# Strassen in the second channel product, affine parts moved, and batch 0 pipelined by head pair, in an attention and ResMLP kernel

## The chip, the cores and the metric

The kernel runs on one core of one Trainium2 chip. The metric is the device time of one execution in microseconds (us), as a median over runs. The span in a profile is some 2 us shorter than that time, since it starts at the core's first instruction. Runs over 1.5% above the fastest of the same kernel are named where they occurred; they count in the medians quoted and not in the ratios.

## The reference

Input q, k, v are 4 batches x 8 heads x 768 tokens x 64. A sorting matrix `P` (8x8 for each head, normalised five times by rows and columns) mixes the 8 blocks of k and v. Attention within each block follows, and its output (768 x 512 for a batch) goes through a ResMLP block.

```python
for _ in range(5):                       # P = sort_net
    P = np.exp(P - P.max(-1, keepdims=True))
    P = P / P.sum(-1, keepdims=True); P = P / P.sum(-2, keepdims=True)
k_sorted = np.einsum('bhij,bhjcd->bhicd', P, k_b)      # v in the same way
x = softmax(scale * q_b @ k_sb^T) @ v_sb               # per block of 96 tokens
a1  = alpha1 * x + beta1
u   = x + lam * np.einsum('ts,bsd->btd', w_tok, a1)    # token mixing, 768 x 768
a2  = alpha2 * u + beta2
out = u + lam * (np.maximum(a2 @ w_ch1, 0.0) @ w_ch2)  # 512 -> 2048 -> 512
```

`lam` is about 0.01, so the channel product contributes little to the output.

## The kernel before

TensorE (`pe`) multiplies, ScalarE (`act`) does the exponentials and ReLUs, VectorE (`dve`) does most evictions (copies of results out of PSUM, where TensorE writes). In the traces below sc_ps are the scores, et their exponentials, x_ps is et times v (`Vs`), k_ps and q_ps are k and q on their way to kT and qT, tok_ps is token mixing, and h_ps and ch_ps are the two channel products. Tokens are kept in tiles of 128, of which 96 rows come from the first six blocks and 32 from the last two. `w_tok` must be transposed with its columns in that order. The kernel before sorts them on VectorE and then transposes full tiles of 128 columns:

```python
def sort_wtok(n):
    ...
    for lo, hi, base in ((0, 96, 0), (96, 128, TAIL)):     # two copies on VectorE
        dve.tensor_copy(t_[:, :, :, lo:hi], wt16[...])

def prep_wtok(which, eng):
    for ks in which:
        pst = psb([128, S], F16, "wtok_ps")
        for tt in range(NT):
            pe.transpose(pst[:, tt * 128:(tt + 1) * 128], wtp[ks // 2][:, tt, ks % 2, :], ident16[:])
        eng(w_tokT[:, ks, :], pst[:])
```

The channel part works on halves of 384 tokens. The first product (`h_ps`) needs a ReLU on ScalarE for each result, the second (`ch_ps`) needs two VectorE operations for each tile of 128 tokens:

```python
def moe_h(b, hf, which=range(HT)):
    for m in which:
        hps = psb([128, 384], FT, "h_ps")
        for ci in range(CT):
            pe.matmul(hps[:], W1p[:, ci, m*128:(m+1)*128], a2T_of[b][hf][:, ci, :], ...)
        act.activation(hT_of[(b, hf)][m], hps[:], AF.Relu)

def moe_ch(b, hf, kks=range(3)):
    ...
        for m in range(HT):
            pe.matmul(cps[:], hT[m][:, kk*128:(kk+1)*128], W2p[:, m, lo:hi], ...)
        dve.tensor_tensor(cps[:], cps[:], lamB[:, lo:hi], ALU.mult)
        dve.tensor_tensor(ost[:, lo:hi], cps[:], u_of[b][kt][:, lo:hi], ALU.add)
```

Where batch 1's attention is prepared, channel products of batch 0 stand between its k and q pieces:

```python
for kk in range(2):
    moe_ch(0, 0, (kk,))
    mix_k(1, gs=((0, 1), (2,))[kk])
    for h4 in range(2 * kk, 2 * kk + 2):
        turn_q(1, h4, dve.tensor_copy)
```

The softmax here doesn't subtract the row's maximum and nothing guards it: scores larger than these inputs give would overflow.

## Time and profile before

| | before |
|---|---|
| median of the first 3 runs | 268.65 us |
| span of the profiled run | 266.8 us |
| TensorE / VectorE / ScalarE busy | 96% / 58% / 47% |
| start of first h_ps (end of the head) | 42.47 us |
| token mixing of batches 1, 2, 3 starts at | 85.09, 143.86, 202.64 us |

I use these points as stage boundaries throughout. "Head" is all before the first h_ps; stage 2 runs from there to token mixing of batch 1; stages 3 and 4 end at token mixing of batches 2 and 3; the last stage ends with the last matmul.

A timeline line gives start, duration, engine, line, operation, names, shapes and count.

```profile
25.55 0.51 PE L65 MATMUL wtok_ps<-ident,wtp 128*128 128x128 f16 x6
```

A run of matmuls lasts 0.16 us beyond its stream (a record of 512 columns lasts 379 ns, and in a full stream the next one starts after 216), so the six here take (0.51 - 0.16) / 6 = 0.058 us each. All 36 cost 3.0 us.

The same timeline in stage 2, and the window around it (stretch, length, then busy time of PE, PEld, DVE, ACT, POOL, then granted clock, DMA share and GB/s):

```profile
55.03 2.75 PE L65 MATMUL ch_ps<-W2p,hTa 128*128 128x512 bf16 x11
57.62 1.03 PE L65 MATMUL ch_ps<-W2p,hTb 128*128 128x512 bf16 x4
58.49 1.06 PE L65 MATMUL k_ps<-bigP,raw 128*128 128x128 f16 x16
59.48 1.00 PE L65 MATMUL q_ps<-ident,qn 128*64 128x128 f16 x24
60.41 2.76 PE L65 MATMUL ch_ps<-W2p,hTa 128*128 128x512 bf16 x11
```

### The profile page before, as it was taken

How to read it: one execution, taken by the hardware profiler on the slowest of the kernel's cores; microseconds unless marked ns; L12 is line 12 of the kernel's file. 1: busy time of each engine (PE TensorE's matmuls, PEld its weight loads, DVE VectorE, ACT ScalarE, POOL GpSimd, SP SyncE). 2: the span in 40 equal slices, each digit the busy share in tenths (PEclk: the TensorE clock that was granted, in tenths of full speed). 3: DMA queues.
4: the chain of work that ended last, by engine and by line, in shares of the span. 5: the costliest groups of instructions: out<-in, count | busy, mean ns of one | idle time of the engine just before them, and what ended most of it. 6: DMA issues, size and time to landing. Idle time of an engine off the chain costs nothing.

```text
span 266.8 us, 5147 instructions
## 1 busy us (share of the span) xinstructions
PE 257.3 (96%) x2049; PEld 141.6 (53%) x2059; DVE 154.8 (58%) x333; ACT 125.8 (47%) x232; POOL 92.6 (35%) x100
## 2 busy tenths in 40 slices
PE   7799999999999999999999999999999999999993
PEld 3467745565565444554565444554565445545542
DVE  6878687639567966722585867704675962042033
ACT  3376767642585312980375404970474305505600
POOL 8524789103585615008918125002409000000000
PEclk9999999999999999999999999999999999999999
DMA  6999999989999544499996342492200422012012
GB/s 80 183 208 252 206 211 207 209 209 118 206 165 146 115 83 120 115 83 95 207 196 135 61 100 80 118 109 51 81 1 2 86 71 79 2 39 79 2 39 79
DMA packets 62423, 30.88 MB, mean 116 GB/s; under 512 B 48888, under 2 KB 58112, under 8 KB 62400
## 3 DMA queue, kind: packets, MB, share of 16 engines
q0 software_dynamic: 23024, 15.60, 39.1%
q1 hardware_dynamic: 39376, 14.96, 32.7%
q8 instruction: 16, 0.26, 0.4%
q14 instruction: 7, 0.06, 0.1%
HBM read 32.78 MB, written 8.65 MB: 155 GB/s over the span
## 4 chain that ended last, share of the span: by engine, by line
PE 89%; ACT 4%; DVE 4%; issue 1%; DMA 1%; DVEq 0%; ACTq 0%
PE ch_ps L65 31%; PE h_ps L65 30%; PE tok_ps L65 12%; PE x_ps L65 5%; PE sc_ps L65 4%; ACT kT L65 2%; PE v_ps L65 2%; PE k_ps L65 1%; PE q_ps L65 1%; ACT et L65 1%; DVE csum L65 1%; DVE P L65 1%; PE m_ps L65 1%; DVE rsum L65 1%; PE wtok_ps L65 1%
## 5 line engine op out<-in xcount | busy, mean ns | idle before, releaser
L65 PE MATMUL h_ps<-a2T,W1p 128*128 128x384 bf16 x512 | 93.4, 326 | 0.2
L65 ACT ACTIVATE hTa<-h_ps 128x384 bf16<-128x384 f32 x96 | 45.9, 492 | 67.7 <-PE h_ps L65 66.6
L65 PE MATMUL ch_ps<-W2p,hTa 128*128 128x512 bf16 (+2 forms) x290 | 65.9, 370 | 0.5
L65 PEld LDWEIGHTS <-W1p 128*128 128x128 bf16 x512 | 47.5, 98 | 30.3 <-issue 0.9
L65 DVE TENSOR_TENSOR ch_ps<-ch_ps,lamB 128x512 f32<-128x512 f32 (+2 forms) x25 | 16.9, 676 | 62.8 <-PE ch_ps L65 60.1
L65 POOL TENSOR_SCALAR u<-b1lB,rs 128x512 f32<-128x512 f32 x18 | 28.9, 1612 | 64.7 <-DVE ost L65 60.1
L65 PEld LDWEIGHTS <-hTa 128*128 128x128 bf16 x300 | 28.7, 98 | 32.4
L65 PE MATMUL tok_ps<-x,w_tokT 128*128 128x512 f16 x144 | 32.1, 379 | 0.0
L65 POOL TENSOR_TENSOR u<-x,u 128x512 f32<-128x512 f16 x22 | 25.4, 1190 | 18.2 <-DVE x L65 17.3
L65 ACT ACTIVATE et<-sc_ps 96x768 f16<-96x768 f32 x32 | 24.9, 807 | 11.7 <-PE sc_ps L65 11.7
L65 ACT CAST u<-u 128x512 f16<-128x512 f32 x24 | 14.8, 618 | 25.7 <-DVE u L65 25.7
L65 PE MATMUL ch_ps<-W2p,hTb 128*128 128x512 bf16 (+2 forms) x100 | 25.0, 371 | 0.0
L65 PEld LDWEIGHTS <-w_tokT 128*128 128x128 f16 x180 | 14.8, 97 | 16.1
L65 DVE TENSOR_TENSOR tok_ps<-tok_ps,a1lB 128x512 f32<-128x512 f32 x24 | 16.6, 693 | 7.7 <-PE tok_ps L65 7.6
L65 DVE CAST kT<-k_ps 64x512 f16<-64x512 f32 x24 | 16.5, 688 | 3.4 <-PE k_ps L65 3.0
L65 DVE TENSOR_TENSOR x<-x_ps,recip 96x512 f16<-96x512 f32 (+2 forms) x32 | 17.6, 554 | 0.9
L65 DVE TENSOR_TENSOR u<-tok_ps,u 128x512 f32<-128x512 f32 x24 | 16.4, 689 | 1.7
L65 ACT ACTIVATE hTb<-h_ps 128x384 bf16<-128x384 f32 x32 | 15.3, 497 | 3.8 <-PE h_ps L65 3.4
L65 DVE TENSOR_TENSOR ost<-ch_ps,u 128x512 f32<-128x512 f32 (+2 forms) x25 | 16.6, 665 | 0.6
L65 POOL DMA_DIRECT2D qn<-in_q_dram x18 | 15.4, 872 | 4.2 <-PE q_ps L65 3.4
L65 PEld LDWEIGHTS <-hTb 128*128 128x128 bf16 x100 | 9.6, 98 | 10.9
L65 PEld LDWEIGHTS <-et 96*128 96x128 f16 (+2 forms) x288 | 12.4, 99 | 4.6 <-issue 1.2
(95 smaller groups left out, 214.0 us busy)
## 6 DMA issues: line engine op xcount, KB each, us to landing
out_dram<-ost SPq DMA_DIRECT2D x23, 192.0 KB, 2.2
raw<-in_v_dram POOLq DMA_DIRECT2D x8, 384.0 KB, 8.2
raw<-in_k_dram POOLq DMA_DIRECT2D x8, 384.0 KB, 10.7
vscr<-vA SPq DMA_DIRECT2D x6, 384.0 KB, 4.4
Vs<-vscr SPq DMA_DIRECT2D x6, 384.0 KB, 7.5
W1p<-in_moe_w_ch_dram POOLq DMA_DIRECT2D x4, 512.0 KB, 10.5
W2p<-in_moe_w_ch_dram POOLq DMA_DIRECT2D x4, 512.0 KB, 18.6
qn<-in_q_dram POOLq DMA_DIRECT2D x12, 128.0 KB, 5.8
```

The source lines that it names most:

```text
L65: ins = getattr(self.eng, name)(*args, **kwargs)
```

## The change

Its intent is to save columns on TensorE: two tiles of tokens become one Strassen product of seven block products instead of eight. The sums of hT blocks and the seven evictions go to VectorE. `lam` is folded into W2, alpha2 into W1, beta2 into a bias of the ReLU, and alpha1 and beta1 are applied to x before token mixing. Batch 0's attention is pipelined by head pair. The operands of both channel products become f16 instead of bf16. The sorting copies of `w_tok` go, and each tile is transposed in two parts, 96 and 32 columns, instead. The core of the diff:

```diff
-    def sort_wtok(n):
...
     def prep_wtok(which, eng):
         for ks in which:
             pst = psb([128, S], F16, "wtok_ps")
             for tt in range(NT):
-                pe.transpose(pst[:, tt * 128:(tt + 1) * 128], wtp[ks // 2][:, tt, ks % 2, :], ident16[:])
+                cols = slice(tt * 128, (tt + 1) * 128)
+                pe.transpose(pst[0:96, cols], wt16[:, tt, 96 * ks:96 * ks + 96], ident16[:])
+                pe.transpose(pst[96:128, cols], wt16[:, tt, TAIL + 32 * ks:TAIL + 32 * ks + 32], ident16[:])
             eng(w_tokT[:, ks, :], pst[:])
...
-    spin(psb([128, 512], FT, "spin_ps")[:], 7)
+    spin(psb([128, 512], FT, "spin_ps")[:], 12)
...
+    def affine(b, lo, hi, eng, kts=slice(0, NT)):
+        eng.tensor_tensor(xa, x, a1l16[...], ALU.mult)
+        eng.tensor_tensor(xa, xa, b1l16[...], ALU.add)
...
+    def moe_h(b, th, which=range(MH)):            # thirds of 256 tokens
+            for mm in range(2):
+                act.activation(hT[:, m, :], hps[:, mm, :], AF.Relu, bias=hbias[:, m:m + 1])
...
+    def moe_sums(b, th):                          # four sums of 128x1024, f16
+        dve.tensor_tensor(S1, A21, A22, ALU.add)
+        dve.tensor_tensor(S2, S1, A11, ALU.subtract)
+        dve.tensor_tensor(A21, A11, A21, ALU.subtract)
+        dve.tensor_tensor(S4, A12, S2, ALU.subtract)
...
+        product(pa, A11, B11, True, False)        # 8 matmuls of 256 columns each
+        take(u11, pa)                             # u += ps / 1024 on VectorE
+        product(pb, A12, B21, True, True)
+        take(u11, pb)
+        product(pa, S2, T2, False, False)
+        take(u12, pa)
...                                               # four more
...
+    for n in range(3):
+        mix_k(1, gs=(n,), share=(2, 0, 2))
+        turn_q(1, n, act.copy)
+        moe_h(0, 1, range(2 + n, 3 + n))
+    turn_q(1, 3, act.copy)
+    for n in range(4):
+        scale_w2(n)                               # 4 x 2048 elements on VectorE
+    combine_w2()                                  # 4 x 2048 elements on VectorE
```

## The prediction

> **What bounds the kernel now.** I read the page first (busy shares, then the chain that ended last), then the timeline of TensorE, then the windows between the points that the timeline gives, then the groups by form for durations.
>
> ```profile
> PE 257.3 (96%) x2049; PEld 141.6 (53%) x2059; DVE 154.8 (58%) x333; ACT 125.8 (47%) x232; POOL 92.6 (35%) x100
> ...
> PE 89%; ACT 4%; DVE 4%; issue 1%; DMA 1%; DVEq 0%; ACTq 0%
> ```
>
> TensorE is busy 96% of the span and is 89% of the chain, mostly ch_ps (31%), h_ps (30%) and tok_ps (12%). So matmul columns are the currency, as long as nobody makes TensorE wait. The timeline of TensorE shows the rate and the stages:
>
> ```profile
> 42.47 4.06 PE L65 MATMUL h_ps<-a2T,W1p 128*128 128x384 bf16 x24
> ...
> 85.09 7.93 PE L65 MATMUL tok_ps<-x,w_tokT 128*128 128x512 f16 x36
> ...
> 241.53 10.56 PE L65 MATMUL h_ps<-a2T,W1p 128*128 128x384 bf16 x64
> ...
> 262.10 0.39 PE L65 MATMUL ch_ps<-W2p,hTb 128*128 128x128 bf16 x4
> ```
>
> One matmul lasts 0.16 us beyond its stream, so 64 of 384 columns in 10.56 us are 162 ns each, and 36 of 512 in 7.93 us are 216 ns each: columns/2.4 plus 2.5 ns. Weight loads hide. The windows, cut at the first h_ps and at the starts of tok_ps:
>
> ```profile
> 33.80:42.47 8.67, 8.67 (x55) 4.20 (x52) 7.14 (x15) 5.79 (x10) 7.78 (x8) 1.00 1.16 210
> 42.47:85.09 42.62, 42.41 (x393) 25.09 (x395) 29.31 (x58) 25.14 (x48) 18.50 (x21) 1.00 1.28 182
> 85.09:143.86 58.77, 58.46 (x418) 30.76 (x419) 35.21 (x72) 28.24 (x53) 25.53 (x26) 1.00 0.92 130
> 143.86:202.64 58.78, 58.47 (x420) 30.71 (x420) 35.11 (x71) 28.25 (x53) 16.43 (x13) 1.00 0.42 71
> 202.64:262.49 59.85, 59.69 (x322) 31.04 (x323) 21.98 (x38) 19.95 (x40) 4.16 (x4) 1.00 0.19 49
> ```
>
> Columns: stretch, length, then busy time of PE, PEld, DVE, ACT, POOL. DVE has 13 us free in the second line and 24 us in the third, but VectorE works in order and the change gives it much more to do. The durations that I price with, from the groups by form:
>
> ```profile
> L65 DVE TENSOR_TENSOR tok_ps<-tok_ps,a1lB 128x512 f32<-128x512 f32 x24 | 16.6, 693 | 7.7 <-PE tok_ps L65 7.6
> L65 DVE CAST kT<-k_ps 64x512 f16<-64x512 f32 x24 | 16.5, 688 | 3.4 <-PE k_ps L65 3.0
> L65 DVE TENSOR_TENSOR x<-x_ps,recip 96x256 f16<-96x256 f32 x12 | 5.0, 418 | 0.3
> L65 ACT ACTIVATE hTa<-h_ps 128x384 bf16<-128x384 f32 x96 | 45.9, 492 | 67.7 <-PE h_ps L65 66.6
> ```
>
> [...] The trace agrees (162 and 216 ns), so 256 columns should take 109 ns. [...]
>
> **The change part by part.**
> *Strassen.* Two token tiles now need 7 products of 8 matmuls of 256 columns instead of 32 matmuls of 512. Per batch: 96 x 216 ns = 20.7 us becomes 168 x 109 ns = 18.3 us. The first channel product goes from 128 x 162 = 20.8 to 192 x 109 = 21.0 us because it now runs in thirds of 256 tokens. Net 2.2 us less per batch, 8.8 us in all. This is the whole gain on TensorE.
> *What it adds on VectorE.* [...] Seven evictions of 256 columns from PSUM: 0.42 us, 0.40 start to start, 84 of them = 34 us; they replace 50 operations of about 0.68 us (33.5 us), so that is even. [...]
> *Affine parts.* W1 carries alpha2 and the ReLU bias carries the rest: 24 operations of 375 ns (7.5 us) on VectorE go, and so do 24 tok_ps multiplications (16.6 us) and the whole POOL preparation. In return x is multiplied and shifted in 16 bits[...], at the worst place: between the last attention tile and token mixing.
> *ScalarE.* 192 ReLUs of 256 instead of 128 of 384. Runs of ScalarE (6 of 384 in 2.53 us, 3 of 768 in 2.20 us) give 0.41 and 0.70 us start to start, so 0.31 us for 256: 0.62 us per pair against 0.87 us of matmuls. Off the path by itself, but batch 1 also moves four q copies (0.70) and four kT copies (0.58) to it.
> *Head.* Two operations of 1x512 join the normalisation loop, where VectorE has 0.4 us of slack per round: about 0.6 us late each, 1.2 us in all. 64 bias matmuls for 36 row sums at 27 ns: +0.8 us. Twice as many w_tok transposes: +1.8 us. Interleaving head pairs fills the 2 to 3 us in which TensorE waited between 11.3 and 33.8. Following the order of the build, first h_ps at 42.9 instead of 42.5.
>
> **By stage, along the order of the build.**
> 1. To the first h_ps: +0.5.
> 2. First h_ps to token mixing of batch 1 (42.6 now). TensorE alone: 21.0 h, 12.2 Strassen, 10 for the rest = 43.2. VectorE alone: u and uT 3.8, masks 1, v copies 3.6, kT 2.8, [...]attention 7.1, gathers 2.7, [...] = 44 us. Two in-order engines, each nearly full, which wait for each other in turn: VectorE idles some 5 us before the first attention tile because ScalarE is late with q and kT[...]. I get 50 to 51: about +8.
> 3. and 4. Token mixing to token mixing (58.8 now, of which 2 are stalls). TensorE 54.6. [...]plus about 2 at kT, exp and evictions. 58.5: -0.3 each.
> 5. Token mixing of batch 3 to the last matmul (59.9 now). 7.8 + 21.0 + 4 x 6.1 = 53.2[...]: 54.6: -5.2.
> 6. Tail: one eviction and one store of 192 KB after the last product: -0.2.
> Sum: 268.65 + 0.5 + 8 - 0.6 - 5.2 - 0.2 = 271.2.
> I do not take all of it. A walk on paper puts waits one after the other, and stage 2 is its largest and least certain term. The buffers, copy shares and warm-up counts of the new kernel look fitted to it, which speaks for fewer waits. I take two thirds of the 8 in stage 2: **268.7 us**.
>
> **Rivals.**
> *TensorE stays the only bound.* Then 268.65 - 8.8 + 0.5 = 260.4, with a few waits 261 to 263. For it: 96% busy now, VectorE at 58%. Against: an eviction has 0.87 us (one product) until TensorE wants the same bank again, and in the trace an eviction starts 0.26 us after the stream ends; with 0.42 us that leaves 0.2 us[...].
> [...]
> *The head pays.* If the earlier loads and head-pair order bring the first h_ps to 39 to 40, 266. For it: DMA is at nine tenths over the first ten slices and loses three broadcasts of 256 KB. Against: q, k and v already come in about when wanted, and the copies per tile are the same.
>
> **Range and chances.** All waits as walked: 271 to 272; with stage 2 worse, 275. Half of the stalls hidden: 265; hardly any: 261 to 263. Range 262.5 to 274. Faster than 263.3 needs the added waits to stay under 3 us, where I count 11: 0.2. Slower than 274: 0.12. Between: 0.68.
>
> **What would show it.** Matmuls of 256 at 109 ns and Strassen blocks of about 6.1 us in the last batch confirm the gain[...]. The stage from first h_ps to token mixing of batch 1 should be the one that grew, with VectorE near full in it; the stages between should be about as long as before; the last one 5 us shorter. The chain should show more VectorE than 4%. I am wrong if TensorE keeps 96% busy with a shorter span[...], or if the first h_ps starts before 40.

Some passages of the record are cut: they were rules and figures that did not come from a trace or run of this case. In the walk of stage 2 the terms of VectorE for W2, the sums and the affine part go (and the evictions that stood beside the last), so the terms left no longer add up to its 44 us. Also cut are a comparison with TensorE behind its +8, a stall of 2 us in stages 3 and 4, a term of the last stage beside its 53.2, and one rival. As recorded, 268.65 + 0.5 + 8 - 0.6 - 5.2 - 0.2 came to 271.2, and 268.7 with two thirds of the 8. The +8, the two -0.3 and the -5.2 rest in part on the cut terms, as my estimates.

Three statements have their figures here. Weight loads hide: PEld is busy 141.6 us with loads of about 98 ns, and matmuls of 512 columns still start every 0.216 us. A matmul of 256 columns at 109 ns follows from the line through 162 ns for 384 and 216 for 512. VectorE and TensorE work in order: in e16 the first sixteen x_ps were done by 71.74 us, and VectorE first read one at 75.36, after the last two operations on W2, queued before, had started at 72.96 and 74.22; in e4 the first x_ps ran at 77.64 us, behind h_ps in TensorE's queue, and in e12, where fewer stood ahead of it, at 73.59.

## More of the kernel before

On the page of the kernel before, the row of TensorE's busy tenths and the row of its granted clock, in 40 slices:

```profile
PE   7799999999999999999999999999999999999993
PEclk9999999999999999999999999999999999999999
```

TensorE is full from the third slice on, at full clock.

```profile
55.00:72.00 17.00, 16.84 (x162) 9.51 (x163) 11.51 (x19) 6.74 (x12) 6.34 (x8) 1.00 1.21 173
```

While ScalarE and VectorE prepare k, q and the first exponentials of batch 1, TensorE works on ch_ps, which asks nothing of ScalarE. It is busy 16.84 of 17 us; ScalarE only 6.74.

The groups by form and the timeline of TensorE show the `w_tok` transposes.

```profile
L65 PE MATMUL wtok_ps<-ident,wtp 128*128 128x128 f16 x36 | 2.9, 220 | 0.1
```

## The result, and the profile after

The changed kernel took 289.34 us (median of 4 runs, 288.59 to 290.66) against 268.77 us of the kernel before (4 runs, 268.57 to 269.89): slower, ratio 1.0761 [1.0712, 1.0811]. Its results are right. A ratio here is the mean time of one kernel's fast runs over the mean of the other's in the same rounds, so it is not quite the ratio of the quoted medians. The profiled run was fast, with a span of 286.8 us: 20.0 us more than before.

From the page of the kernel after, the busy shares, TensorE's busy tenths and granted clock, and the chain of waits by engine:

```profile
PE 271.2 (95%) x2693; PEld 206.6 (72%) x2693; DVE 177.8 (62%) x384; ACT 146.8 (51%) x303; POOL 37.2 (13%) x54
...
PE   8999999998879988999999999999999899999994
...
PEclk9999965999999999999999999999999999999999
...
PE 70%; DVE 13%; ACT 13%; issue 2%; POOL 0%; ACTq 0%; POOLq 0%; DVEq 0%
```

TensorE fell from 89% to 70% of the chain; VectorE and ScalarE rose to 13% each. And in the sixth and seventh slice the granted clock fell to 6 and 5 tenths, though TensorE is marked full. The windows between the boundaries of the kernel after (the columns are as above):

```profile
13.75:48.25 34.50, 33.83 (x456) 22.77 (x455) 17.96 (x40) 14.36 (x22) 10.71 (x13) 0.84 1.21 209
48.25:58.27 10.02, 10.01 (x88) 8.10 (x84) 4.46 (x7) 1.98 (x4) 0.00 (x0) 0.87 0.67 112
58.27:111.65 53.38, 47.47 (x529) 38.30 (x529) 42.82 (x81) 34.79 (x74) 8.46 (x11) 1.00 0.99 100
...
228.69:282.69 54.00, 53.73 (x454) 44.12 (x451) 23.86 (x48) 23.86 (x54) 0.00 (x0) 1.00 0.20 55
```

| stage | before | after | difference | walked in the prediction |
|---|---|---|---|---|
| head, to first h_ps | 42.47 | 58.27 | +15.80 | +0.5 |
| 2, to token mixing of batch 1 | 42.62 | 53.38 | +10.76 | +8 |
| 3, to token mixing of batch 2 | 58.77 | 58.16 | -0.61 | -0.3 |
| 4, to token mixing of batch 3 | 58.78 | 58.88 | +0.10 | -0.3 |
| last, to the last matmul | 59.85 | 54.00 | -5.85 | -5.2 |
| tail | 4.31 | 4.11 | -0.20 | -0.2 |
| span | 266.8 | 286.8 | +20.0 | +2.5 |

So the loss is in the head and in stage 2. In the head, TensorE's timeline and the groups by form show the transposes of `w_tok` (a merged timeline line names the form of its first instruction only):

```profile
26.68 2.15 PE L66 MATMUL wtok_ps<-ident,W2T 128*96 128x128 f16 x12
...
36.95 2.87 PE L66 MATMUL wtok_ps<-ident,W2T 128*96 128x128 f16 x12
40.64 5.95 PE L66 MATMUL wtok_ps<-ident,W2T 128*96 128x128 f16 x24
...
48.25 8.67 PE L66 MATMUL tok_ps<-xa,w_tokT 128*128 128x256 f16 x66
```

```profile
L66 PE MATMUL wtok_ps<-ident,W2T 128*96 128x128 f16 x36 | 10.7, 297 | 0.0
L66 PE MATMUL wtok_ps<-ident,W2T 128*32 128x128 f16 x36 | 9.3, 257 | 0.0
```

72 transposes take 15.3 us where 36 took 3.0: at full clock about 0.17 us each ((2.15 - 0.16) / 12), at the reduced clock 0.24 ((5.95 - 0.16) / 24). They show up as busy time, not as a wait, and so the busy share of TensorE stayed at 95%.

In stage 2, two stretches tell how it went. The first is while k and q of batch 1 are prepared, and answers to the window of 17 us shown of the kernel before. The second is just before token mixing:

```profile
72.00:86.00 14.00, 11.46 (x147) 9.05 (x143) 11.14 (x12) 13.63 (x26) 6.84 (x8) 1.00 1.56 117
...
101.00:111.65 10.65, 8.66 (x74) 6.94 (x74) 10.55 (x24) 0.00 (x0) 0.00 (x0) 1.00 0.28 75
```

ScalarE is busy 13.63 of 14 us in the first, VectorE 10.55 of 10.65 in the second, and TensorE is idle for 2.5 and 2.0 us of them (5.9 us in the whole stage). In the last stage the matmuls run at the rate that the prediction took, 109 ns for 256 columns ((14.14 - 0.16) / 128). The stage also holds one tile of channel product less than before, which moved to stage 2, so its -5.85 us is not all Strassen's:

```profile
236.46 1.04 PE L66 MATMUL ch_a<-W2p,hT 128*128 128x256 f16 x8
...
241.70 1.04 PE L66 MATMUL ch_a<-W2T,hT 128*128 128x256 f16 x8
242.57 14.14 PE L66 MATMUL h_ps<-uT,W1p 128*128 128x256 f16 x128
```

Seven products take 242.57 - 236.46 = 6.11 us. Three VectorE and ScalarE groups by form give what a ReLU, an eviction and a sum cost:

```profile
L66 ACT ACTIVATE hT<-h_ps,hbias 128x256 f16<-128x256 f32 x192 | 77.8, 490 | 25.0 <-PE h_ps L66 23.4
L66 DVE SCALAR_TENSOR_TENSOR u<-ch_a,u 128x256 f32<-128x256 f32 x48 | 20.1, 421 | 8.3 <-PE ch_a L66 8.3
L66 DVE TENSOR_TENSOR S<-hT 128x1024 f16<-128x1024 f16 x12 | 8.3, 691 | 35.6 <-ACT hT L66 35.6
```

### The profile page after: what moved, and what is told of

Same layout as the page of the kernel before. It is cut to its first block, busy times and chain, and to the rows that moved or that the text cites. A ratio compares the mean times of both kernels' runs of the same rounds, so it can differ in the third digit from the quotient of the medians.

```text
span 286.8 us, 6448 instructions
## 1 busy us (share of the span) xinstructions
PE 271.2 (95%) x2693; PEld 206.6 (72%) x2693; DVE 177.8 (62%) x384; ACT 146.8 (51%) x303; POOL 37.2 (13%) x54
## 4 chain that ended last, share of the span: by engine, by line
PE 70%; DVE 13%; ACT 13%; issue 2%; POOL 0%; ACTq 0%; POOLq 0%; DVEq 0%
PE h_ps L66 19%; PE tok_ps L66 11%; PE ch_a L66 11%; PE ch_c L66 6%; PE wtok_ps L66 5%; ACT hT L66 5%; PE sc_ps L66 4%; PE spin_ps L66 3%; PE x_ps L66 3%; DVE x L66 3%; DVE u L66 3%; ACT et L66 3%; DVE xa L66 3%; ACT kT L66 2%; DVE S L66 2%
## 5 line engine op out<-in xcount | busy, mean ns | idle before, releaser
L66 PE MATMUL h_ps<-uT,W1p 128*128 128x256 f16 x768 | 92.9, 273 | 2.5 <-ACT hT L66 1.1
L66 ACT ACTIVATE hT<-h_ps,hbias 128x256 f16<-128x256 f32 x192 | 77.8, 490 | 25.0 <-PE h_ps L66 23.4
L66 PEld LDWEIGHTS <-W1p 128*128 128x128 f16 x832 | 74.4, 98 | 14.1 <-issue 2.9
L66 PEld LDWEIGHTS <-hT 128*128 128x128 f16 x384 | 37.2, 98 | 6.9 <-issue 1.8
L66 PEld LDWEIGHTS <-S 128*128 128x128 f16 x288 | 27.8, 98 | 8.0 <-issue 3.1
L66 PE MATMUL tok_ps<-xa,w_tokT 128*128 128x512 f16 (+1 forms) x180 | 33.3, 347 | 0.0
L66 PE MATMUL ch_a<-W2T,hT 128*128 128x256 f16 x192 | 25.4, 272 | 1.3 <-DVE u L66 1.3
L66 PE MATMUL ch_c<-W2p,S 128*128 128x256 f16 x192 | 26.2, 273 | 0.4 <-DVE S L66 0.2
L66 DVE SCALAR_TENSOR_TENSOR u<-ch_a,u 128x256 f32<-128x256 f32 x48 | 20.1, 421 | 8.3 <-PE ch_a L66 8.3
L66 DVE SCALAR_TENSOR_TENSOR u<-tok_ps,x 128x512 f32<-128x512 f32 x24 | 16.2, 689 | 12.8 <-PE tok_ps L66 12.0
L66 PE MATMUL wtok_ps<-ident,W2T 128*96 128x128 f16 x72 | 15.3, 277 | 0.0
L66 PEld LDWEIGHTS <-et 96*128 96x128 f16 (+2 forms) x288 | 12.3, 100 | 3.5 <-issue 1.3
```

The costliest lines, as they stand in the source:

```text
L66: ins = getattr(self.eng, name)(*args, **kwargs)
```

## The experiments

Eighteen kernels ran, each for three timed rounds besides the profile. The first eight took the parts of the change apart; the last ten went after stage 2. Times are medians of all four runs.

### The head: e1, e2, e3, e4, e8

**e1_grouped.** The same 72 transposes in another order: six of 96 columns, then six of 32.

```diff
             for tt in range(NT):
                 cols = slice(tt * 128, (tt + 1) * 128)
                 pe.transpose(pst[0:96, cols], wt16[:, tt, 96 * ks:96 * ks + 96], ident16[:])
+            for tt in range(NT):
+                cols = slice(tt * 128, (tt + 1) * 128)
                 pe.transpose(pst[96:128, cols], wt16[:, tt, TAIL + 32 * ks:TAIL + 32 * ks + 32], ident16[:])
```

> The changed kernel with only the order of the w_tok transposes altered: per block first the six of 96 columns, then the six of 32. In the changed kernel they alternate and a block of 12 takes 2.15 us, 0.18 us each; the 36 full ones of the kernel before took some 0.06 us each. Theory A (each change of the column width between two neighbouring transposes makes the array finish the first before the second starts): 2 changes per block in place of 12, a block takes 0.7 to 1.0 us, the granted clock stays at 1.00, first h_ps at about 46 instead of 58.3, time 276 to 279. Theory B (transposes of partial width are slow in themselves, or the strided stationary operand is): no change, 288 to 290. Theory C (the drop of the granted clock comes first and slows them): blocks before the drop keep 2.15 us, so at most 3 us gained.

Measured: 277.73 us (one of four runs slow, 281.79), ratio to before 1.0373 [1.0294, 1.0452]. That is 11.6 us less than the changed kernel, by order alone. TensorE's timeline of e1:

```profile
26.35 0.97 PE L66 MATMUL wtok_ps<-ident,W2T 128*96 128x128 f16 x12
...
34.58 1.88 PE L66 MATMUL wtok_ps<-ident,W2T 128*96 128x128 f16 x24
```

A block of twelve takes 0.97 instead of 2.15 us, the last two blocks 1.88 instead of 5.95, and the granted clock stays at 1.0 throughout. First h_ps moved from 58.27 to 46.72. Stages 2 to 4 and the last agree with the changed kernel within 0.02 us, so nothing else moved. That the array finishes one width before the next starts was Theory A's guess at a reason; what the run shows is the cost of the alternation.

**e2_quads.** All parts 32 columns wide: every transpose goes to another 32-row group of the result than its neighbour, but all have the same width.

```diff
-                pe.transpose(pst[0:96, cols], wt16[:, tt, 96 * ks:96 * ks + 96], ident16[:])
+                for n in range(3):
+                    lo = 96 * ks + 32 * n
+                    pe.transpose(pst[32 * n:32 * n + 32, cols], wt16[:, tt, lo:lo + 32], ident16[:])
```

> The changed kernel with each 96-column transpose cut into three of 32, so that all 144 transposes have one width but neighbouring ones go to different column groups. Theory A (a change of width drains): no width changes, so 24 transposes take about 0.7 to 1.3 us per block, time 276 to 280. A rival form of A (any change of the destination column group drains): 24 x 0.18 = 4.3 us per block, time about 300 or more. Theory B (partial width slow in itself): slower than 289.

Measured: 281.04 us (one of four slow, 287.47), ratio 1.0416. On e2's timeline a block of 24 transposes takes 0.52 us:

```profile
30.08 0.52 PE L66 MATMUL wtok_ps<-ident,W2T 128*32 128x128 f16 x24
```

So going to another row group costs nothing here (the 24 x 0.18 = 4.3 us of the rival form did not come); it is the change of width that costs. It even gains: (0.52 - 0.16) / 24 is 0.015 us each, a quarter of 0.058, and in the single records of this block four transposes start within 0.01 us of each other. So neighbours of the same width of 32 that go to different row groups start together here. The run was not faster than e1 all the same, and above the 276 to 280 expected: TensorE paused with no releaser in the trace for 2.34 us before token mixing, and again for 3.18 us in stage 2 (at 90.67 us), which made that stage 2.8 us longer. The fast runs scattered from 278.6 to 282.7 us. I have no explanation for these pauses.

**e3_before_split.** The kernel before, with its full-width transposes split into 96 and 32 columns alternately. If the alternation is the cause, it must slow down the kernel before, too.

```diff
-                pe.transpose(pst[:, tt * 128:(tt + 1) * 128], wtp[ks // 2][:, tt, ks % 2, :], ident16[:])
+                cols = slice(tt * 128, (tt + 1) * 128)
+                pe.transpose(pst[0:96, cols], wtp[ks // 2][:, tt, ks % 2, 0:96], ident16[:])
+                pe.transpose(pst[96:128, cols], wtp[ks // 2][:, tt, ks % 2, 96:128], ident16[:])
```

> The kernel before with one part of the change alone: each full w_tok transpose cut into one of 96 and one of 32 columns, alternating. If this is what the change lost before the first h_ps, the six blocks grow from about 0.5 to 2.15 us each, in sum about 10 us, plus 2 to 3 if the granted clock falls: 278 to 282. If the loss belongs to the new order of batch 0, 269 to 271.

Measured: 286.51 us (286.14 to 287.59), ratio 1.0656 [1.0631, 1.068]. This one part makes the kernel before 17.4 us slower, more than the 278 to 282 us expected. The timeline of e3, and its granted clock in 40 slices:

```profile
33.97 5.92 PE L65 MATMUL wtok_ps<-ident,wtp 128*96 128x128 f16 x24
41.57 5.95 PE L65 MATMUL wtok_ps<-ident,wtp 128*96 128x128 f16 x24
```

```profile
PEclk9999555699999999999999999999999999999998
```

The same 5.95 us for 24, and the same fall of the clock, here over four slices. After the first h_ps the stages are those of the kernel before (42.62, 58.79, 58.80, 59.85).

**e4_grouped_spin5.** e1 with the last warm-up block (matmuls whose result nobody reads) cut from 12 to 5: in the changed kernel the normalised P is ready at 12.27 us, but the warm-up matmuls ahead in TensorE's queue end at 13.75.

```diff
-    spin(psb([128, 512], FT, "spin_ps")[:], 12)
+    spin(psb([128, 512], FT, "spin_ps")[:], 5)
```

> The grouped order of e1, and 5 warm-up matmuls in place of the last 12. In the changed kernel the normalisation ended at 12.3 us and the warm-up matmuls at 13.75. If they hold up the head: 1.4 us under e1. If what comes later waits for the loads or for ScalarE and VectorE anyway: same as e1.

Measured: 276.16 us (276.09 to 278.89), ratio 1.0289 [1.0242, 1.0337]: 1.6 us less than e1. First h_ps at 45.81. By its median this is the fastest kernel with right results and all parts of the change (the intervals of e6 and e8 overlap with its), and it is the base of most experiments below.

**e8_quads_spin5.** e2 with the same cut.

```diff
-    spin(psb([128, 512], FT, "spin_ps")[:], 12)
+    spin(psb([128, 512], FT, "spin_ps")[:], 5)
```

> Four transposes of 32 columns each as in e2, where a block took 0.5 us against 0.97 in e1, with 5 warm-up matmuls as in e4. If the blocks stand on the path: 6 x 0.45 = 2.7 us under e4, 273 to 274. If the pause of 2.3 us in e2, for which the profile names no releaser, comes again: 275 to 279 with a spread of several us between runs.

Measured: 277.45 us (275.42 to 278.32), ratio 1.0247 [1.0138, 1.0357]. The head is 0.42 us shorter than in e4, and stage 2 is 2.0 us longer. The pauses without a releaser came again, 1.29 us before token mixing and 2.39 us in stage 2 (at 86.88 us), and they take up what the faster transposes gave. Inconclusive as a gain.

### What Strassen is worth: e5

**e5_plain.** e4 with plain products instead of Strassen (same thirds, `lam` in W2), no sums, no combination of W2.

```diff
-        product(pa, A11, B11, True, False)
-        take(u11, pa)
...
+            for m in range(HT):
+                pe.matmul(
+                    cps[:], hT[:, m, kk * 128:(kk + 1) * 128], W2p[:, m, :], start=(m == 0), stop=(m == HT - 1),
+                )
             with tc.high_priority():
+                dve.scalar_tensor_tensor(u[:], cps[:], 1.0 / LAM_UP, u[:], op0=ALU.mult, op1=ALU.add)
...
-    combine_w2()
```

> The kernel of e4 (276.2) with the second channel product done plainly again: 32 matmuls of 512 columns per two token tiles, one eviction each, no sums, no combinations of W2; everything else of the change stays. Strassen saves 2.4 us of matmuls per batch. Theory D (in the stages that also hold attention its sums and evictions cost VectorE as much as it saves): first h_ps to token mixing of batch 1 gets 2 to 5 us shorter, the two stages after that stay within 1 us, the last one gets 2 to 4 us longer: 273 to 278 in all. Theory E (it pays all over): every stage longer, 284 to 286.

Measured: 279.81 us (278.93 to 280.69), ratio 1.0352. By the medians Strassen is worth 279.81 - 276.16 = 3.65 us, by the profiled spans 3.0 (277.4 and 274.4); the two ran in different batches, and their ratios to the kernel before (1.0352 and 1.0289) put it at 1.7. By stages of the profiled runs the plain kernel is 1.66 us shorter in stage 2, and 1.4, 0.7 and 2.5 us longer in the other three: neither theory's range. By columns Strassen saves 20.7 - 18.3 = 2.4 us in each batch, 9.6 in all, and by any of the three figures less than half of that reaches the end.

### Stage 2: which engine sets it? e6, e7, e9, e10, e11

All are e4 with one load taken from an engine. "Stage 2" is from the first h_ps to token mixing of batch 1; the second figure is to token mixing of batch 2, which helps where the order around token mixing changed (e10 starts it with four matmuls and the rest 1.7 us later; in e10 and e11 the first matmul of the next one, some 3 us ahead of the rest, is left out).

| kernel | to token mixing 1 | to token mixing 2 | run |
|---|---|---|---|
| before | 42.62 | 101.39 | 268.77 |
| e4_grouped_spin5 | 53.39 | 111.56 | 276.16 |
| e6_q_on_dve | 52.94 | 112.74 | 277.38 |
| e7_no_shift | order changed | 111.20 | 274.68 |
| e9_q_dve_no_w2 | 52.94 | 112.77 | 277.84 |
| e10_relu512 | 52.8 | 111.97 | 276.70 |
| e11_all | 51.71 | 111.68 | 276.17 |

The granted clock has to be read beside this table, since in some of these runs it fell to 0.50 for 3.4 us where it stayed at 1.00 in e4. In e6, e9 and e11 that was at the start of token mixing of batch 1 (98.6 to 102.1 us in e6), after TensorE had waited 2.6 us for VectorE. It leaves the first figure alone and adds to the second and to the run. In e10 it was inside stage 2, from 96.2 to 99.7 us, after a wait of 3.22 us. In e10, e11 and e14 it fell in the head as well, and the first h_ps came at 47.1 to 47.2 us instead of 45.8.

**e6_q_on_dve.** The four q copies of batch 1 move from ScalarE to VectorE, as in the kernel before.

```diff
-        turn_q(1, n, act.copy)
+        turn_q(1, n, dve.tensor_copy)
...
-    turn_q(1, 3, act.copy)
+    turn_q(1, 3, dve.tensor_copy)
```

> The kernel of e4 with the four q copies of batch 1 on VectorE, as in the kernel before, in place of ScalarE. In the changed kernel ScalarE is busy 12.0 of 12.1 us in the stretch before the first attention tile of batch 1. Theory F (ScalarE sets that stretch): 4 x 0.7 us less on it, the stage to token mixing of batch 1 gets 2 to 3 us shorter, 273 to 274.5. Rival (VectorE sets the whole stage): 2 us more on VectorE, same or up to 2 us longer, 276 to 278.

Measured: 277.38 us, ratio 1.0263 [1.018, 1.0345]. Stage 2 fell by 0.45 us only. The next stage grew by 1.6 us, which is about what 3.4 us at half the clock cost.

**e7_no_shift.** Wrong (relative error 0.029): the addition of beta1 to x is left out, which takes the second of two steps from VectorE's path to token mixing.

```diff
-        eng.tensor_tensor(xa, xa, b1l16[:, lo:hi].unsqueeze(1).to_broadcast(shape), ALU.add)
```

> The kernel of e4 without the addition of beta1 to the input of token mixing: wrong by a small term on purpose. It takes away 1.35 + 0.55 us of VectorE per later batch between the last attention tile and token mixing, nothing else. Theory D (VectorE holds up token mixing there): about 1.5 us less in each of three stages, 271 to 272.5. Rival (TensorE has other work meanwhile): 276.

Measured: 274.68 us (273.88 to 275.36), ratio 1.0161. Only 1.5 us less in all, and in the profiled run 0.9: 0.4 us up to token mixing of batch 2 and 0.5 in stage 4.

**e9_q_dve_no_w2.** Wrong, though it passes the comparison because `lam` is small: e6 without the eight operations on W2.

```diff
-    T1, (T2, T3, T4) = B12, (W2T[:, n] for n in range(3))
+    T1, (T2, T3, T4) = B12, (B11, B21, B22)
...
-    for n in range(4):
-        scale_w2(n)
-    combine_w2()
```

> Wrong result on purpose: e6_q_on_dve without the scaling and the combination of W2 on VectorE, eight operations of 2048 elements, 9.5 us; the Strassen products read unprepared W2. In e6 the stage from the first h_ps to token mixing of batch 1 took 52.9 us. Theory A, VectorE and ScalarE bound this stage in turn: with 9.5 us taken from VectorE, q copies on VectorE no longer cost it anything and ScalarE stays the bound until about 85 us, so the stage falls to 49 to 51. Theory B, the W2 work lies in time in which VectorE waits for ScalarE anyway: the stage stays within 0.5 us of e6.

Measured: 277.84 us (277.21 to 278.44). Stage 2 is 52.94 us, to the hundredth that of e6. In this order, 9.5 us of VectorE work lay wholly in time in which VectorE waits.

**e10_relu512.** Wrong on purpose (passes, since beta2's contribution is small): one ReLU of 512 columns without bias.

```diff
-            for mm in range(2):
-                m = 2 * n + mm
-                act.activation(hT[:, m, :], hps[:, mm, :], AF.Relu, bias=hbias[:, m:m + 1])
+            act.activation(hT[:, 2 * n:2 * n + 2, :], hps[:], AF.Relu)
```

> Wrong result on purpose: e4_grouped_spin5 with one ReLU of 512 columns without bias in place of two of 256 with their bias columns. In e4 a pair takes 0.74 us start to start (18 in 6.84 us with the tail). Theory A, ScalarE bounds the stretch from 60 to 80 us: a 512-column ReLU takes 0.55 us, 24 pairs give back some 4 us of ScalarE, and the stage of 53.4 us falls by 2 to 3.5 us. The later stages change by less than 0.5. Theory B, ScalarE is late because of the order in which its pieces are queued: the stage falls by under 1 us.

Measured: 276.70 us (275.41 to 277.59). The group took 603 ns each, 0.53 us start to start in a run of six (3.25 us); the 0.55 of the expectation was an estimate. ScalarE got its time back, and stage 2 fell by 0.6 us: under the 1 us that the expectation gave as the mark against a plain ScalarE bound. But the clock was at half for 3.4 us of this stage, which can hide up to 1.7 us (an estimate: half of that time). So e10 alone does not rule Theory A out. It does show where the time went: ScalarE had finished the stage's exponentials by 85 us, and VectorE was busy for all of 90 to 95 us while TensorE waited.

**e11_all.** e9 and e10 together (edits as there).

> Wrong result on purpose: e9 and e10 together (q copies on VectorE, no work on W2, one ReLU of 512 columns without bias). Theory A, two bounds in turn: each relief alone is partly wasted, so together they give more than the sum of e9 and e10; stage 2 falls from 53.4 to 46 to 48, near the 43.2 us of TensorE's own work. Theory B, VectorE after the last attention tile (copies, xa, evictions, sums, 87 to 99 us) is the bound whatever ScalarE does: 49 to 51.

Measured: 276.17 us (one of four slow, 280.81). Stage 2 is 51.71 us: neither theory's range. TensorE now hardly paused up to 90 us, and stopped at the end instead. From e11's timeline of TensorE, token mixing of batch 1 (the bracket gives the idle time before and what ended it):

```profile
98.78 9.62 PE L66 MATMUL tok_ps<-xa,w_tokT 128*128 128x512 f16 x36 [2.59 <-DVE xa L66]
```

VectorE, which had idled 5.5 and 4.6 us before the first attention tile at 78 us, was then full until this point. The first tile came so late because 74 h_ps matmuls stood ahead of the first x_ps in TensorE's queue.

### Stage 2: order and filler. e12 to e18

| kernel | to token mixing 1 | to token mixing 2 | run | clock fell in stage 2 |
|---|---|---|---|---|
| e12_pv_early | 54.12 | 113.00 | 277.20 | yes |
| e13_combine_late | mixed | 114.51 | 279.06 | yes |
| e14_pv_early_no_w2 | 54.25 | 113.11 | 277.81 | yes |
| e15_early_all | 50.51 | 109.09 | 272.93 | no |
| e16_early_q_dve | 56.37 | 115.23 | 279.31 | yes |
| e17_ch_first | 50.00 | 109.05 | 273.45 | no |
| e18_plain_first | 57.33 | 116.20 | 279.98 | yes |

**e12_pv_early.** Right result: TensorE's queue is fixed so that scores and x_ps of each head pair stand between pairs of h_ps.

```diff
             cur = [emit_scores(b, h4, g) for g in range(2)]
+            fill(1)                       # one pair of h_ps, batch 1 only
             emit_pv(b, h4 - 1, prev, x128, xs)
+            fill(2)
...
-    pe.fixed = False
...
+        pe.fixed = False                  # now after the attention of batch 1
```

> Right result: e4_grouped_spin5 with one change of order in batch 1: TensorE's queue is fixed so that the scores and x_ps of each head pair come between pairs of h_ps, instead of 43 h_ps matmuls standing between the last early scores and the first x_ps. In e4 the first exp ended at 70.5 us, Vs had come by 72, and the first x_ps ran at 77.6; VectorE was idle 1.8 us before it and had some 21 us of work after it until token mixing. Theory A, the queue order sets the stage: the first x_ps comes at 72 to 73, VectorE goes straight from W2 to the tiles at 74.3, and the stage falls from 53.4 to 49 to 50.5. Theory B, VectorE's total load sets it, W2 included: it falls by less than 1.5 us.

Measured: 277.20 us (276.91 to 277.59). The first x_ps came at 73.59 instead of 77.64, and VectorE went straight from W2 to the tiles, as expected. But stage 2 did not get shorter. The windows of e12 tell why:

```profile
65.00:70.00 5.00, 3.10 (x36) 2.04 (x35) 4.97 (x5) 4.92 (x10) 3.25 (x4) 0.82 1.81 118
70.00:75.00 5.00, 4.31 (x44) 3.41 (x44) 4.79 (x6) 4.33 (x8) 5.00 (x8) 0.50 1.91 127
```

TensorE had nothing to do for 1.9 us while ScalarE was full, and the granted clock fell to half, for 6.8 us in all: eight h_ps matmuls took 1.89 instead of 1.05 us. What the order gave, the pauses and the clock took back.

**e13_combine_late.** Right result: e12 with the four combining steps of W2 spread between the head pairs.

```diff
     def fill_h(n):
+        if n == 2:
+            combine_w2(steps.pop(0))      # one step of 2048 elements
         if todo:
```

> Right result: e12 with the four steps that combine W2 (1.23 us each) placed one after each head pair's tiles instead of before all. Theory A, order: the first tiles start when x_ps is there, at 72 instead of 74.3, and the stage is 1 to 2 us shorter than in e12. Theory B, VectorE's total load sets the stage: within 0.7 us of e12, since only the order of the same work changes.

Measured: 279.06 us (278.36 to 279.68): 1.9 us slower than e12. One matmul of token mixing came 52.87 us after the first h_ps, the rest at 55.84. Both theories missed.

**e14_pv_early_no_w2.** Wrong: e12 without the work on W2 (edit as in e9).

> Wrong result on purpose: e12 without the scaling and combination of W2 on VectorE (9.5 us). Theory A, order alone: like e13, the tiles start when x_ps is there; the stage is 48 to 49. Theory B, VectorE's total load: the stage falls well below e12, by 4 us or more, to 45 to 47, where TensorE's 43.2 us and the start-up of the stage remain.

Measured: 277.81 us (one of four slow, 282.95). Stage 2 is 54.25 us, no shorter than e12: in this order VectorE's load is not the bound, since it idled 9.6 us before the first tile. The clock was at half for 6.8 us here too (69.9 to 76.7 us). Both theories missed.

**e15_early_all.** Wrong: e14 with the q copies on VectorE and the ReLU of 512 (edits as in e6 and e10).

> Wrong result on purpose: e14 (scores and x_ps between pairs of h_ps, no W2 work on VectorE) with the q copies on VectorE and one ReLU of 512 columns without bias. Theory A, the stage has two limits in a row, ScalarE's pieces before the first attention tiles and VectorE's tail after them, and each of the changes so far took away only one: with both away the stage falls from 53.4 to 46 to 48.5 us, near TensorE's 43.2. Theory B, something else holds it (the way of v through memory, or the halved clock after TensorE's waits): it stays at 50 or more.

Measured: 272.93 us (272.10 to 274.76), ratio 1.0150 [1.01, 1.0201]. Stage 2 is 50.51 us. That is 1.2 us less than e11, which has the same relief in the old order and also kept its clock in this stage, and 2 us short of the expected 48.5. The 3.7 us to e14 are in part e14's fallen clock. Before the first x_ps TensorE now waited 1.22 us for v, which comes back through memory.

**e16_early_q_dve.** Right result: e12 with the q copies on VectorE (edit as in e6).

> Right result: e12 with the four q copies on VectorE (0.56 us each there, 0.70 start to start on ScalarE). In e12 ScalarE was full from 60 to 70 us and the first exp came at 69.8. Theory A: ScalarE is 2.8 us earlier with the first exp, TensorE's pauses between 65 and 72 us shrink, the stage falls from 54.1 to 51 to 52.5. Theory B: as e6 was to e4, less than 0.7 us.

Measured: 279.31 us (279.00 to 281.16): 2.1 us slower than e12. The scores came earlier, and then TensorE stopped for 3.80 us behind VectorE, which was busy with W2, and the clock fell to half. A miss.

**e17_ch_first.** Wrong: e14 with the first Strassen block between the k and q pieces of batch 1, where the kernel before has its channel product.

```diff
+    moe_sums(0, 0)
+    steps = moe_ch_steps(0, 0)            # moe_ch, cut after products 2, 4 and 6
     for n in range(3):
         mix_k(1, gs=(n,), share=(2, 0, 2))
         turn_q(1, n, act.copy)
-        moe_h(0, 1, range(2 + n, 3 + n))
+        next(steps)
     turn_q(1, 3, act.copy)
+    for _ in steps:
+        pass
```

> Wrong result on purpose: e14 (new order of scores and x_ps, W2 not prepared) with the first Strassen block, 7 products that need no ScalarE, between the k and q pieces of batch 1, and the three pairs of h_ps that stood there moved behind. ScalarE and VectorE keep all their other work. Theory A, TensorE's filler in that stretch must not depend on ScalarE: ScalarE is 2.2 us earlier with the first exp, TensorE has 6.1 us of products while it waits, the stage falls from 54.3 (e14) to 46 to 49. Theory B, the way of v through memory and the attention itself set the stage: 51 or more.

Measured: 273.45 us (one of four slow, 280.50), ratio 1.0141 [1.0094, 1.0187]. Stage 2 is 50.00 us: 4.25 us less than e14 with the same load on every engine, though 1 us above the expected range. The window of e17 over these pieces, and that of e4 over the same stretch:

```profile
59.00:75.00 16.00, 14.67 (x194) 12.03 (x192) 9.49 (x20) 12.76 (x22) 5.86 (x10) 1.00 1.18 132
```

```profile
59.00:75.00 16.00, 13.47 (x169) 10.80 (x167) 12.52 (x14) 15.63 (x31) 8.30 (x11) 1.00 1.61 129
```

TensorE is busy 14.67 instead of 13.47 us, and ScalarE is no longer full (12.76 against 15.63). The clock stayed at 1.00. A large part of the 4.25 us can be that: e14's 6.8 us at half the clock cost up to 3.4 us (an estimate, half of that time). Runs that kept their clock in this stage compare better. With ScalarE's and VectorE's other loads left as they were, e17 is as fast as e15, which had both relieved (50.51), and 2.9 us faster than e9, which also lacks W2's preparation (52.94). Against both, other things differ too: the order of scores and x_ps against e9, the place of the q copies against both.

**e18_plain_first.** Right result, the candidate: e12 with the first two tiles of batch 0 as plain products at that place, because plain products need no combined W2, and W2 prepared after them.

```diff
+            for m in range(HT):
+                pe.matmul(cps[:], hT[:, m, kk * 128:(kk + 1) * 128], W2p[:, m, :], ...)
+            dve.tensor_tensor(cps[:], cps[:], lam16[:], ALU.mult)
+            dve.scalar_tensor_tensor(u[:], cps[:], 1.0 / LAM_UP, u[:], op0=ALU.mult, op1=ALU.add)
```

> Right result, a candidate: e12 with the first two tiles of batch 0 as plain products (32 matmuls of 512 columns, 6.9 us instead of 6.1, with lam at the eviction) between the k and q pieces of batch 1, and W2 scaled and combined on VectorE after them. Theory A: the stage falls from 54.1 (e12) to 47.5 to 50, the run to 270 to 273, still not under the kernel before (269). Theory B: 52 or more, run 275 or more.

Measured: 279.98 us (279.79 to 280.13), ratio 1.0393. Stage 2 is 57.33 us. TensorE's timeline of e18 at the second pair of scores:

```profile
80.29 0.56 PE L66 MATMUL sc_ps<-qT,kT 64*96 64x96 f16 x8 [5.19 <-DVE x L66]
```

W2's preparation now ran from 71.2 to 81.3 us, just when the first tiles came. TensorE waited 5.19 us for a PSUM buffer behind it, and the clock fell to half during that pause. So W2's 9.5 us, which cost nothing where e9 and e14 took them away, hold TensorE up as soon as the first x_ps comes before they are done, as in e16 and e18.

No version that gives right results beat the kernel before. The best is e4 with 276.16 us, a loss of 2.9%.

## Why the prediction was wrong

It said 268.7 us (262.5 to 274) and the kernel took 289.3. The gain on TensorE came as priced, and stage 2 was rightly named as the stage that grows; one term of the head was wrong by far, and stage 2 was booked at two thirds of 8 us and cost 10.8.

**The step that failed** is "Twice as many w_tok transposes: +1.8 us". The 36 more transposes took 12.3 us more (15.3 against 3.0), and pulled the granted clock down with them, which added 1.3 us to the first part of token mixing (66 matmuls in 8.67 us; 7.37 in e4). I had priced a transpose by its columns alone. What the runs show is a cost of each change of width. With 0.058 us for a transpose and 0.16 us for the end of a block, the twelve of a block leave (2.15 - 0.16 - 12 x 0.058) / 11 = 0.12 us for each of eleven changes. In e1 there is one change in a block, and (0.97 - 0.16 - 0.70) / 1 = 0.11 us; in the double block three, and (1.88 - 0.16 - 1.39) / 3 = 0.11 us. The figure is worked out, not read off, but it is the same three times. The records of the weight loads fit it. In e1 the next load starts as soon as a matmul of the same width has begun, and the twelve loads of a block take 0.80 us. In the changed kernel each load starts 0.16 to 0.19 us after the matmul before it, and the twelve take 2.01 us. The price also stood in the kernel before: each of its x_ps blocks goes from six matmuls of 128 columns to six of 32, and at 19.94 us this one step takes 0.12 us from start to start where the others take 0.03 to 0.04. I had read the new lines as transposes and expected nothing of a change of width. The runs show the price of the change, not its inner reason; that something drains, as the expectation of e2 puts it, was not shown. The price of 1.8 us would have been near for the grouped order: 5.8 us in e1, 2.8 more than before.

**The fall of the clock** came with the alternation and left with it (e1: 1.0). In stage 2 it fell to exactly 0.50 in e12 from 70 to 75 us, after pauses of at most 1 us each, and in e18 during one of 5.19 us. Yet e4 had pauses of 0.99 and 1.09 us and kept its clock, and so did e2 after one of 3.18 and e8 after one of 2.39. What decides it, no run here shows.

**The other terms of the head.** "About 0.6 us late each, 1.2 us in all" for the normalisation: e4 starts the first matmuls that need the finished P 1.17 us after the kernel before (12.51 against 11.34), right. The bias matmuls: +0.8 predicted, 1.75 against 1.05 us for the row sums, right. The warm-up matmuls in front, 12 instead of 7, I had not priced: 1.6 us by the runs of e1 and e4, 0.9 by their spans (275.3 and 274.4). "Interleaving head pairs fills the 2 to 3 us": e4 needs 24.58 us where the kernel before needed 22.46, and 2.8 + 0.7 us of that are the two items above, so about 1.4 us was filled. This is worked out as what remains.

**Stage 2** was walked as +8 and came as +10.8; "I take two thirds of the 8" was the wrong way. That ScalarE is late first and VectorE holds token mixing up last is what the trace shows. But VectorE was not near full (42.8 of 53.4 us), and W2's preparation, which the walk counts in its 44 us and which takes 9.5 us, cost nothing (e9), so that 8 walked comes near 10.8 measured is partly luck. Two terms were too small: the ReLU with bias goes at 0.37 us start to start (18 in 6.84 us), where I took 0.31 from groups without a bias; and I took TensorE's filler as given. A single one with bias takes 490 ns for 256 columns here, and one of 512 without bias 603 in e10. The experiments show that no single load sets the stage: 9.5 us off VectorE (e9), some 4 us off ScalarE (e10), both (e11) and the order alone (e12) gave at most 1.7 us, though the fallen clock hides part of e10 and e12. What gave more was order with both loads off (e15, 2.9 us), and a channel product in the place where the kernel before has it (e17, 3.4 us, without W2's preparation). The likely reason is the filler: TensorE's only other work there, h_ps, asks for a ReLU of the very engine that is late. e17 speaks for it but does not show it, since no run changes the filler alone at an undisturbed clock. The channel product asks for nothing of ScalarE, but in Strassen's form it needs W2 combined and hT summed first. What is left of the stage in e17, 50.0 us against 42.6, stays open, but for 1.8 us: the stage now holds four tiles of channel product in Strassen's form (14 products of 0.873 us) where it held three plain ones (48 of 216 ns). The last stage has one tile less for the same reason.

**Stages 3, 4 and the last** were right: 58.2 and 58.9 against 58.5 walked, 54.0 against 54.6, Strassen blocks of 6.1 us. Sums of 1024 f16 elements take 691 ns and W2's steps of 2048 take 1224, so 0.52 ns for each further element; evictions from f32 PSUM take 421 ns for 256 and 689 for 512, so 1.05 ns. The two-tensor operations on f16 run at twice that rate. Two small points of the working do not hold: the sum with two thirds of the 8 is 268.5 and not 268.7; and the 2 us of stalls in stages 3 and 4 of the kernel before are not in its window lines, where TensorE is idle for 0.3 us. The last stage's agreement also rests on its having one tile less, which the walk had counted. The changed kernel reads a partial sum in the middle of an accumulation group, and that costs nothing visible: 421 ns, as the 418 ns of an eviction of like size before.

**The rivals.** "TensorE stays the only bound" fell: its share of the chain is 70%. "The head pays" fell by its sign. The range failed because it was drawn around stage 2 and had no place for a mispriced instruction in the head. Without the two repaired faults of the head, the kernel is at 276.2, still 2.2 us outside.

## What to carry to other kernels

Price an instruction in its neighbourhood, not by its columns alone: here two transposes of different output width cost 0.12 us more at each change, and grouping them leaves one change for each block. Look at what fills TensorE's queue while another engine is late: work that needs that same engine is a poor filler (likely here, not shown), and fewer columns help only where TensorE is the one that others wait for. Compare stages only after a look at the granted clock of each. A saving should be booked in the stage where it falls: against plain products, Strassen gained 2.5 us in the last stage, where nothing competes with TensorE, and lost 1.7 us in stage 2.
